# Sliding-window attention and a gated MLP on one core: one explicit order of steps for every engine, and weights loaded by casting DMA

## The chip, the cores and the metric

The kernel runs on one core of one Trainium2 chip. The metric is the device time of one execution in microseconds. Each version was run several times beside the kernel before on the same chip, and only runs in the fast state are compared. A ratio is the mean time of one kernel's fast runs over that of the other's of the same rounds, so it is not quite the ratio of the medians that are quoted, and its 95% interval stands behind it in brackets. The kernel before had medians of 200.6 to 201.8 us in the different calls. So versions are compared by ratio, or by starts and spans within the traces.

Engines are named as in the profile: PE (TensorE matmul), PEld (its weight loads), DVE (VectorE), ACT (ScalarE), POOL (GpSimd), SP (SyncE, which here only issues DMAs).

## The reference, cut to what matters

```python
# q, k, v: (4, 8, 768, 64) float32; n_sink = 4, window = 128
rel  = pos[:, None] - pos[None, :]
keep = (pos[None, :] < n_sink) | ((rel >= 0) & (rel < window))
a    = softmax(where(keep, q @ k.T / 8, -1e9)) ;  x = a @ v        # x: (4, 768, 512)
h    = gelu_tanh(x @ w_in)                                         # w_in: (512, 1024)
u, v = h[..., :512], h[..., 512:]
v_n  = (v - mean(v)) / sqrt(var(v) + 1e-6) * g_ln
v_s  = w_sg @ v_n + b_sg                                           # over the 768 positions
out  = x + (u * v_s) @ w_out                                       # w_out: (512, 512)
```

There are four batches. Each has four pairs of heads, so there are 16 times three inputs of 384 KB each (18.9 MB in all). The weights w_in, w_sg and w_out are 2, 2.25 and 1 MB as float32. The outputs are 6.3 MB.

## The kernel before

For each batch b there is an attention part, pair by pair: cast q, k and v to bf16, transpose on PE (`trp`), scores (`sc`), exponentials on ACT, masks on DVE or POOL, products with v (`av`). Then comes a feed-forward part: `hv` (called MV), `hu` (MU), layer norm of v into `z`, the spatial product `vs` (SP), a gate, and the output `ops`. The spatial product and the output of batch b are mixed with the attention of batch b+1.

```python
def T(b, p):                                   # one pair's inputs: cast, transpose, copy
    for name, src in (("q", q32), ("k", k32)):
        ...
        if name == "k" and b >= 2: nc.scalar.copy(cv, sv)
        else:                      pcast(cv, sv)                 # POOL
        ps = ps_mm.tile([128, NT, 128], BF16, name="trp", tag="mm")
        for t in range(NT): nc.tensor.transpose(ps[:, t, :], ..., iden)
        ...
    pcast(v_sb[b % 2][...], v32...)
...
def load_w_sg(ti):                             # 6 of these; w_in and w_out alike, cast on POOL
    t = wst.tile([128, S], F32, name="wst")    # a pool of 4 buffers
    nc.sync.dma_start(out=t, in_=moe_w_sg[128 * ti:128 * (ti + 1), :])
    r = zpool.tile([128, S], BF16, name="wsg_row")
    nc.vector.tensor_copy(r, t)                # the cast, on DVE
    ...                                        # six transposes on PE, one copy on DVE
...
for b in range(B):
    if b == 0:
        load(1, 0)
        for ti in range(NT): load_w_sg(ti)
        load_vectors(); load(1, 1)
        for c in range(KU): load_w_out(c)
        load(1, 2); load(1, 3)
    for jj in range(NG): MV(b, jj)
    for d in range(KU):
        MU(b, d)
        if b == 0: T(1, d)                     # batch 1's inputs, among batch 0's hu
    if nxt: VS(b + 1)                          # the v_sink product of the next batch, POOL
    su = s_units(b)                            # SP and OUT of batch b
    SK(b + 1, list(range(HP)))                 # sink scores: want all four pairs of b+1
    ...                                        # attention of b+1, with su spread among it
```

The attention of batch 0 is in a fixed order; after it a scheduler orders each engine's instructions.

The softmax here doesn't subtract the row's maximum and nothing guards it: scores larger than these inputs give would overflow.

## Time and profile before

The median was 200.39 us (200.15 to 202.23, three runs). The profiled execution took 202.63 us and spans 200.9 us from its first to its last instruction. To see where it goes, I cut the span at two events per batch, read from the timeline of PE: the first `hv` matmul and the first `vs` matmul.

| stretch | before, us | PE busy in it, us |
|---|---|---|
| start to first hv of batch 0 | 31.2 | 16.6 |
| hv 0 to vs 0 | 33.9 | 23.6 |
| vs 0 to hv 1 | 27.3 | 25.9 |
| hv 1 to vs 1 | 13.0 | 12.0 |
| vs 1 to hv 2 | 29.1 | 26.6 |
| hv 2 to vs 2 | 11.9 | 11.8 |
| vs 2 to hv 3 | 24.1 | 22.8 |
| hv 3 to vs 3 | 10.6 | 10.6 |
| vs 3 to end | 19.9 | 13.8 |

The first two rows stand out: 65 us in which PE is busy for 40. The page of the kernel before shows the same in its 40 slices of 5 us. Each digit is tenths of the slice; PEclk is the granted TensorE clock, DMA the busy share of the DMA engines:

```profile
PE   0458756899067999979988989999999997997992
PEclk9999999999955799999999999999999999999999
DMA  5999993799999502998993002121000122100034
GB/s 171 293 294 329 396 299 136 181 303 319 310 287 299 166 3 64 269 269 254 286 287 64 0 24 84 54 108 52 0 0 5 52 108 100 56 3 2 20 138 157
```

Slice 11 (50 to 55 us) has PE at 0, and then PEclk reads 5, 5, 7. (PEclk also shows 9 where the trace has no clock event yet: the first one is at 16.9 us, and before it six transposes take 0.82 us, as at half clock.) DMA runs at about 300 GB/s up to 65 us, with one dip at 30 to 40 us. The timeline of PE of the kernel before around that hole follows (start, length, line, what, and in brackets the idle time before it and its releaser):

```profile
47.03 2.76 PE L306 MATMUL hu<-xT,w_in_sb 128*128 128x384 bf16 x16
50.69 0.38 PE L213 MATMUL sc<-qT,kT 64*128 64x256 bf16 x3 [0.57 <-ACT uT L148]
55.65 0.82 PE L179 MATMUL trp<-iden,qb 128*128 128x128 bf16 x6 [4.58 <-POOL qb L164]
63.18 0.82 PE L179 MATMUL trp<-iden,kb 128*128 128x128 bf16 x6 [1.09 <-POOL kb L164]
65.07 0.85 PE L319 MATMUL vs<-wsgT,z 128*128 128x384 bf16 x2
```

PE ends batch 0's `hu` before 50 us and waits 4.58 us for an input of batch 1. When it starts again, six transposes take 0.82 us, against 0.50 us when it is warm.

Why the loads are late is seen in the timeline of SP's queue in the kernel before (the length is the time the queue is held by these issues):

```profile
18.30 0.42 SPq L76 DMA_DIRECT2D v_568<-in_v_dram  x1
19.30 16.62 SPq L352 DMA_DIRECT2D wst<-in_moe_w_sg_dram  x6
36.99 0.43 SPq L72 DMA_DIRECT2D q_644<-in_q_dram  x1
39.12 6.30 SPq L364 DMA_DIRECT2D wst<-in_moe_w_out_dram  x4
45.52 0.38 SPq L72 DMA_DIRECT2D q_662<-in_q_dram  x1
```

Six loads of w_sg hold the queue for 16.6 us. The first issue alone takes 7.1 us; 7.4 us pass before the fifth and sixth, which wait for one of four buffers (the queue's own waits there are 3.8 us behind DVE, which makes the casts, and 2.7 us behind the loads before). The inputs of batch 1's second pair stand behind them, and those of the third pair also behind the four loads of w_out.

### The profile page before, as it was taken

What the parts mean: (1) busy time and instruction counts of PE and PEld (TensorE: products, weight loads), DVE (VectorE), ACT (ScalarE), POOL (GpSimd) and SP (SyncE); (2) the same over time, 40 slices, a digit from 0 to 9 for tenths busy, and PEclk for the clock granted to TensorE, in tenths of its full rate; (3) what the DMA queues carried; (4) which work ended last, traced back from release to release, by engine and by line L of the source; (5) the groups of instructions that cost most, each with busy time, mean ns of one, the idle gap of its engine ahead of it and who ended that gap; (6) DMA issues with size and microseconds to landing.
All of it is one profiled execution on the core that took longest, in us unless ns stands there. A gap on an engine that the chain in (4) does not pass through costs nothing.

```text
span 200.9 us, 3839 instructions
## 1 busy us (share of the span) xinstructions
PE 163.7 (81%) x1460; PEld 92.3 (46%) x1460; DVE 140.5 (70%) x269; ACT 112.3 (56%) x131; POOL 110.4 (55%) x173
## 2 busy tenths in 40 slices
PE   0458756899067999979988989999999997997992
PEld 0227533565033566555444446564545655463440
DVE  4148898994855379784756998875759987475653
ACT  2256874557555265758569865646687653761000
POOL 3896597016966689772245995600349651033650
PEclk9999999999955799999999999999999999999999
DMA  5999993799999502998993002121000122100034
GB/s 171 293 294 329 396 299 136 181 303 319 310 287 299 166 3 64 269 269 254 286 287 64 0 24 84 54 108 52 0 0 5 52 108 100 56 3 2 20 138 157
DMA packets 39843, 31.35 MB, mean 156 GB/s; under 512 B 26640, under 2 KB 34832, under 8 KB 39824
## 3 DMA queue, kind: packets, MB, share of 16 engines
q1 hardware_dynamic: 39408, 30.68, 52.5%
q10 hardware_dynamic: 416, 0.43, 0.7%
q8 instruction: 11, 0.18, 0.4%
q14 instruction: 8, 0.07, 0.1%
HBM read 24.81 MB, written 6.29 MB: 155 GB/s over the span
## 4 chain that ended last, share of the span: by engine, by line
PE 31%; DVE 23%; POOL 17%; DMA 11%; issue 8%; ACT 5%; SPq 1%; POOLq 1%; DVEq 0%; ACTq 0%
PE vs L319 10%; DVE pt L221 6%; PE ops L332 6%; DVE z L296 6%; DMA k_646<-in_k_dram 4%; POOL rs L294 4%; PE hv L279 4%; DMA v_1703<-in_v_dram 3%; DVE gtmp L323 3%; PE sc L213 3%; POOL gatedT L326 2%; DMA q_98<-in_q_dram 2%; DVE x_sb L260 2%; POOL kb L164 2%; PE xps L268 2%
## 5 line engine op out<-in xcount | busy, mean ns | idle before, releaser
L326 POOL TENSOR_TENSOR gatedT<-gtmp,uT 128x384 bf16<-128x384 bf16 x32 | 31.4, 984 | 18.1 <-DVE gtmp L323 17.7
L319 PE MATMUL vs<-wsgT,z 128*128 128x384 bf16 x192 | 38.8, 336 | 2.4 <-DVE z L296 1.9
L148 ACT ACTIVATE pt<-sc 128x1024 bf16<-128x1024 f32 (+1 forms) x36 | 32.9, 957 | 6.5 <-PE sc L213 3.6
L323 DVE SCALAR_TENSOR_TENSOR gtmp<-vs,g_sb,b_bc 128x384 bf16<-128x384 f32 x32 | 19.6, 614 | 12.9 <-PE vs L319 12.3
L332 PE MATMUL ops<-w_out_sb,gatedT 128*128 128x512 bf16 x96 | 25.2, 380 | 2.6 <-POOL gatedT L326 2.6
L185 ACT COPY kT<-trp 128x768 bf16<-128x768 bf16 x16 | 12.9, 805 | 23.3 <-PE trp L179 23.3
L319 PEld LDWEIGHTS <-z 128*128 128x128 bf16 x192 | 17.7, 100 | 17.6 <-issue 4.8
L279 PE MATMUL hv<-w_in_sb,xT 128*128 128x512 bf16 x96 | 23.5, 379 | 1.2 <-ACT xT L269 0.9
L213 PE MATMUL sc<-qT,kT 64*128 64x256 bf16 x192 | 19.1, 282 | 4.7 <-ACT pt L148 1.6
L306 PE MATMUL hu<-xT,w_in_sb 128*128 128x384 bf16 x128 | 21.9, 326 | 0.9 <-ACT vt L148 0.9
L290 DVE BATCH_NORM_STATS2 st<-vt 128x6 f32<-128x512 f32 x24 | 15.8, 675 | 9.7 <-ACT vt L148 9.2
L296 DVE TENSOR_SCALAR z<-vt,mv,rs 128x512 bf16<-128x512 f32 x24 | 14.4, 642 | 10.7 <-POOL rs L294 10.6
L221 DVE TENSOR_TENSOR pt<-pt,mask_122 128x1024 bf16<-128x1024 bf16 (+1 forms) x20 | 17.7, 891 | 5.3 <-ACT pt L145 3.9
L269 ACT COPY xT<-xps 128x768 bf16<-128x768 bf16 x16 | 12.9, 804 | 13.8 <-PE xps L268 13.7
L335 DVE TENSOR_TENSOR ot<-ops,x_sb 128x512 f32<-128x512 f32 x24 | 16.3, 687 | 5.1 <-PE ops L332 4.8
L221 DVE TENSOR_TENSOR pt<-pt,mask_127 128x1024 bf16<-128x1024 bf16 x16 | 14.9, 934 | 6.5 <-ACT pt L148 3.4
L292 POOL TENSOR_SCALAR rs<-mv 128x2 f32<-128x2 f32 x12 | 2.3, 193 | 31.1 <-DVE mv L291 30.9
L179 PE MATMUL trp<-iden,qb 128*128 128x128 bf16 x96 | 9.3, 242 | 11.3 <-POOL qb L164 11.2
L260 DVE TENSOR_TENSOR x_sb<-av,rcp 128x384 bf16<-128x384 f32 x32 | 17.6, 556 | 0.9
L183 DVE COPY qT<-trp 128x768 bf16<-128x768 bf16 x16 | 15.1, 944 | 4.3 <-PE trp L179 4.2
L244 PEld LDWEIGHTS <-pt 128*128 128x128 bf16 x192 | 15.2, 100 | 5.4 <-DVE pt L221 3.5
L306 PEld LDWEIGHTS <-w_in_sb 128*128 128x128 bf16 x128 | 12.4, 98 | 9.6 <-issue 1.2
(126 smaller groups left out, 297.8 us busy)
## 6 DMA issues: line engine op xcount, KB each, us to landing
out_dram<-ot SPq DMA_DIRECT2D x24, 256.0 KB, 2.1
wst<-in_moe_w_sg_dram SPq DMA_DIRECT2D x6, 384.0 KB, 5.4
wt<-in_moe_w_in_dram SPq DMA_DIRECT2D x4, 512.0 KB, 7.7
wst<-in_moe_w_out_dram SPq DMA_DIRECT2D x4, 256.0 KB, 4.7
k_100<-in_k_dram ACTq DMA_DIRECT2D x1, 384.0 KB, 4.9
q_98<-in_q_dram SPq DMA_DIRECT2D x1, 384.0 KB, 4.5
v_102<-in_v_dram SPq DMA_DIRECT2D x1, 384.0 KB, 6.3
q_104<-in_q_dram SPq DMA_DIRECT2D x1, 384.0 KB, 6.8
```

What stands on the lines that cost most here:

```text
L148: r = nc.scalar.activation(func=func, **kw)
L213: nc.tensor.matmul(sc[:, hl, 256 * jl:256 * jl + n], kT[b, p][rows, 128 * j:128 * (j + 1)], qT[b, p][rows, 128 * j:128 * j + n], start=Tru ...
L221: nc.vector.tensor_mul(pt[:, :, 0:w], pt[:, :, 0:w], m.unsqueeze(1).to_broadcast([128, 2, w]))
L260: nc.vector.tensor_mul(x_sb[b][:, 3 * half:3 * half + 3, 128 * p:128 * (p + 1)].rearrange("p t (h d) -> p t h d", h=2), av[:, :, :, 0:Dh], ...
L279: nc.tensor.matmul(hp[:, jl, :], xT[b][:, c, 128 * j:128 * (j + 1)], w_in_sb[:, c, d_half:2 * d_half], start=(c == 0), stop=(c == KD - 1))
L296: nc.vector.tensor_scalar(out=z[b][:, 2 * jj + jl, :], in0=vt[:, jl, :], scalar1=mv[:, jl, 0:1], scalar2=rs[:, jl:jl + 1], op0=ALU.subtrac ...
L306: nc.tensor.matmul(hp[:, hf, 0:NH], w_in_sb[:, c, 128 * dc:128 * (dc + 1)], xT[b][:, c, NH * hf:NH * (hf + 1)], start=(c == 0), stop=(c == ...
L319: nc.tensor.matmul(ps[:, 0:NH], z[b][:, si, 128 * dc:128 * (dc + 1)], wsgT[:, si, NH * hf:NH * (hf + 1)], start=(si == 0), stop=(si == NT ...
L323: nc.vector.scalar_tensor_tensor(out=tmp, in0=ps[:, 0:NH], scalar=g_sb[:, dc:dc + 1], in1=b_bc[:, NH * hf:NH * (hf + 1)], op0=ALU.mult, op ...
L326: nc.gpsimd.tensor_mul(gatedT[b, hf][:, dc, :], tmp, uT[b][:, dc, NH * hf:NH * (hf + 1)])
L332: nc.tensor.matmul(ps, gatedT[b, hf][:, dc, 128 * tl:128 * (tl + 1)], w_out_sb[:, dc, :], start=(dc == 0), stop=(dc == KU - 1))
L335: nc.vector.tensor_add(ot, ps, x_sb[b][:, t, :])
```

## The change

The intent: the scheduler is turned off; one list of 713 short words gives each engine's order for the whole program (a word's letter picks the engine, where there is a choice). The weights come by three DMAs issued from POOL that cast float32 to bf16 on the way, so the staging buffers and the casts on engines go. The loads of batch 1 are held until the cast of q of batch 0's last pair, "weights go first". And 32 identity matmuls (WARM) run on PE while it awaits the first q. The list also changes things: three outputs (O, OA, ST 3 to 5) of each of batches 0 to 2 move behind the next batch's first hv; all four `v_sink` products (VS) go to the start.

```diff
+ORDER = """
+Lq00 Lk00 CONST Lv00 Lvs WARM VS0:d VS1:p VS2:p Cq00:p Lq01 Ck00:p Tq00 Lk01 Eq00:a VS3:p Tk00 Ek00:a Lv01 Cv00:p
+...
+Lk03 X011 Ek02:d Cv02:p Lv03 N001 X012 QK020 Iwin KS02:d XT00 X020 M011:d SK02 QK021 Cq03:p M012:d EX00:a AV010
+QK022 M020:d AV011 Ck03:p XS02 Tq03 N010 X021 Tk03 Eq03:d Cv03:p Ek03:a N011 Lq10 Iwsg X022 QK030 KS03:d XT01 M021:d
+...
+M032:d AV030 Lk10 Eq10:d AV031 Lv10 N030 WT0 N031 WT1 WT2 EW0:d XT03 Ck10:p Lq11 EW1:d WT3 EX03:a EW2:d WT4 Lk11
+MV00 EW3:d EW4:d Cv10:p Lv11 MV01 Iwo GV00 Cq11:p WT5 Ck11:p Tk10 EW5:d Tq11 GV01 MV02 BS00 Lq12 Cv11:p Ek10:a Lk12
+...
+KS21:p Cq23:p Ck23:a MV11 GV10 Cq30:p Lk31 Cv30:p O03 Lq32 O04 GV11 BS10 Cv31:p Lk32 MV12 Lv32 BS11 PW10 MU10 GV12
+...
+"""
+    ctx.enter_context(tc.manual_schedule())
...
+    def Iwsg(e):
+        nc.gpsimd.dma_start(out=wsg_rows, in_=moe_w_sg.rearrange("(c p) f -> p c f", p=128))   # f32 -> bf16
...
+    def behind_weights(d, b, p):
+        if (b, p) == (1, 0):
+            tc.add_manual_dep(d.ins, last["Cq", 0, HP - 1].name, ..., reason="weights go first")
...
+    def WARM(e):
+        for _ in range(32):
+            nc.tensor.matmul(ps[:, 0:128], iden, iden, start=True, stop=True)
...
-    def load_w_sg(ti): ...          # staging, cast on DVE
-    def load_w_in(c): ...           # staging, cast on POOL
-    def load_w_out(c): ...
...
+    for word in ORDER.split():
+        what, _, e = word.partition(":")
+        name = what.rstrip("0123456789")
+        steps[name](e, *(int(c) for c in what[len(name):]))
```

In a word, digits are batch, pair, and block. L loads, C casts, T transposes, E copies to SBUF, X exponentials, M masks, EX copies x transposed, WT and EW are the transposes of w_sg and their copies, I are the casting loads, and the other names are as above.

## The prediction

> **What bounds the kernel now.** Reading the span (200.9 us) by the starts of the five stretches, from the timeline (first matmul into hv per batch): 37.3, 92.6, 134.5, 170.4, end 200.9. So the head takes 37 us, then batches cost 55, 42 and 36 us, and the tail 30. The work is the same each time, so the first two periods carry about 19 and 6 us that the third does not.
> Why: the queue of loads (SP) is shared by inputs and weights, and loads stand behind weight buffers: in the windows DMA moves only 145 GB/s at 30-35 us against about 300 around it. In the wait list POOL's qb waits once for 10.7 us behind PE, and PE's transposes wait 11.2 us for qb. PE is busy 0.49 of 5 us at 50-55 us. The granted clock then reads 0.50 at 55-65 and 0.69 at 65-70. Batch 1's transposes come only at 55.7-63.2 us. In the second period POOL and ACT wait for v_1583, v_1703 and k_1701.
> In the third period, PE is busy 23.8 of 25 us (145-170): close to PE-bound.
>
> **What the change does.**
> - Removes: six wsg casts on DVE (3.8 us), four w_in and four w_out casts on POOL (7.9 us). Six of 16 kT/qT copies net leave DVE (16 to 10, 0.94 us each, 5.7 us); ACT gains six copies but sheds three kb casts; POOL sheds four small ks_sink products, gains three kb casts.
> - Adds: three casting loads issued by POOL, 32 identity matmuls at the start.
> - Moves: everything. Loads of batch 1 go after the weights, but no load waits for a weight staging buffer; half of each batch's output matmuls and adds move into the next feed-forward stage, where DVE has room.
>
> **Costing by stage.**
> - Head: 37.3 to about 37. DVE work there falls by about 4 us, but POOL now makes two v_sink tiles (1.06 us each) before the first qb; their vs_all lands at about 7.2 us against q at 5.3, so the start slips by up to 4 us. The spatial weight transposes stand before the first hv on PE and wait for the casting load (estimate 34-36 us: 11 MB at 300 GB/s). No gain.
> - First period: 55 to about 38.5. Inputs through batch 1 are about 15 MB, at 300 GB/s in by 51-53 us instead of 60; the 5 us hole and the half-clock stretch (11.6 us of PE busy at 55-70, so about 5 us) go.
> - Second: 42 to 37.5, less load waiting, outputs deferred.
> - Third: 36 to 34.5. Tail: 30 to 30.
>
> Sum 177.5 us; predicted 178 us, range 171 to 188. Chances: faster 0.94, same 0.04, slower 0.02.
>
> **Warm-up matmuls.** The Trainium skill, "TensorE: Matmul & The Clock Gate" (HAM clock gate), says that the array runs at half rate until about 3.4 us of activity, and again after an idle window. The trace agrees: six transposes take 0.82 us at 6-15 us, 0.50 from 19 us, 0.82 again at 55.7 after the idle 5 us. I give the warm-up under 1 us: PE is idle again before the first qb, and loads bound the head.
>
> **What would show it.** Right: first hv matmuls near 37, 75, 113, 148 us; no clock dip near 50-70; DMA at about 300 GB/s without the hole to 52 us; DVE busy about 10 us lower.
> **What would make it wrong.** Casting loads slower than 300 GB/s, or sharing the DMA engines unfairly (the Trainium skill, "DMA: Bandwidth & Descriptors", arbitration: round robin by packet; no run yet shows it), so that batch 1's inputs or wsg come late and PE, in fixed order, stands before the weight transposes and cools; a fixed order that blocks an engine behind a late item; descriptor writing on POOL costing microseconds.

## More of the kernel before

(In batch 0 of the kernel before, six of the 24 `hv` matmuls come early, from 31.18 us; the other 18 run from 37.32 us on.)

The clock events of the trace put the half clock at 54.5 to 68.1 us. The first `vs` comes only at 65.07; the sink scores, which want all four pairs of batch 1, stand before it.

The q of the third pair (q_662) landed at 50.96 us, just as PE ran out of work, and was cast only from 54.59 us. POOL's timeline of the kernel before shows what stood in front of that cast:

```profile
50.59 1.37 POOL L164 TENSOR_SCALAR w_out_sb<-wst 128x512 bf16<-128x512 f32 x2
52.75 0.62 POOL L164 TENSOR_SCALAR w_out_sb<-wst 128x512 bf16<-128x512 f32 x1
54.01 0.62 POOL L164 TENSOR_SCALAR w_out_sb<-wst 128x512 bf16<-128x512 f32 x1
54.59 1.00 POOL L164 TENSOR_SCALAR qb<-q_662 128x768 bf16<-128x768 f32 x1
```

Between these lines POOL does small steps of the layer norm and of the sink scores. The fourth pair is alike: its k (k_670) landed at 56.5 us and was cast at 62.3. So in the hole it is the order of work on POOL that comes last.

## The result, and the profile after

The changed kernel took 185.81 us in the median (185.32 to 186.25, four runs), against 200.64 us of before in the same rounds: ratio 0.9248 [0.9188, 0.9308]. The profiled run spans 184.3 us. It lies in the predicted range, 7.8 us above the predicted 178. The profiled run of the kernel before was 2.0 us above its median and that of the changed kernel 0.4 us, so the spans differ by 16.6 us, the medians by 14.8; about 1.8 us of the table below are the choice of runs.

| stretch | before | after | difference |
|---|---|---|---|
| start to hv 0 | 31.2 | 40.6 | +9.4 |
| hv 0 to vs 0 | 33.9 | 14.0 | -19.9 |
| vs 0 to hv 1 | 27.3 | 23.6 | -3.7 |
| hv 1 to vs 1 | 13.0 | 15.0 | +2.0 |
| vs 1 to hv 2 | 29.1 | 22.9 | -6.2 |
| hv 2 to vs 2 | 11.9 | 14.6 | +2.7 |
| vs 2 to hv 3 | 24.1 | 21.6 | -2.5 |
| hv 3 to vs 3 | 10.6 | 13.4 | +2.8 |
| vs 3 to end | 19.9 | 18.7 | -1.2 |
| sum | 200.9 | 184.3 | -16.6 |

Up to the first spatial product 10.5 us were gained (65.1 to 54.6), and 6.1 us after it. Put another way: PE is idle for 37.2 us before and 24.9 us after (span less busy time), and its busy time fell from 163.7 to 159.4 us; 12.3 and 4.3 make the 16.6. The busy time fell although WARM adds 3.6 us. PE was busy for 9.8 us at half clock between 54.5 and 68.1 us before and for 5.8 us in the dip of the kernel after, which makes some 2 us of it (an estimate, half of the difference); the rest is not explained by these views.

The page of the kernel after, the same rows as before:

```profile
PE   6047578869989999999999998999989899999971
PEclk9999957999999999999999999999999999999999
DMA  5999699999999968899850022000400120013044
GB/s 159 305 292 275 82 231 199 272 258 279 280 279 307 294 187 223 250 272 316 206 194 0 4 82 91 3 0 0 174 0 0 71 104 4 0 57 114 2 171 171
```

The hole at 50 to 55 us and the half clock behind it are gone. There is a new dip of the clock in slices 6 and 7 (the clock events say half from 23.5 to 30.3 us), a dip of DMA to 82 GB/s in the fifth slice (18.4 to 23.0 us), and a 0 in the second slice of PE.

Three things in the head are new. First, what follows are the waits of the kernel after within its first 12 us (engine, line, releaser: total us, times, longest):

```profile
PE trp L243 <- POOL qb L115: 5.7, 1, 5.7
POOL v_sink_114 L261 <- DMA vs_all<-in_v_dram: 4.4, 1, 4.4
```

POOL must do two v_sink products before the first cast, and they wait for `vs_all`. The first cast starts at 9.9 us, against 5.33 us in the kernel before. The timeline of PE of the kernel after shows what became of the warm-up:

```profile
1.42 3.59 PE L223 MATMUL warm<-iden 128*128 128x128 bf16 x32 [1.42 <-POOL iden masks.py:199]
10.75 0.82 PE L243 MATMUL trp<-iden,qb 128*128 128x128 bf16 x6 [5.73 <-POOL qb L115]
```

PE is idle 5.73 us after it, and the first transposes take 0.82 us, as cold as in the kernel before. In this trace the clock events show no full clock before 16.6 us, so WARM did not even lift it here.

Second, POOL's timeline of the kernel after, and third, DVE's in the same stretch:

```profile
18.46 0.97 POOL L158 DMA_DIRECT2D w_in_sb<-in_moe_w_in_dram  x1
19.46 0.84 POOL L115 TENSOR_SCALAR qb<-q_318 128x768 bf16<-128x768 f32 x1
20.26 0.83 POOL L115 TENSOR_SCALAR kb<-k_351 128x768 bf16<-128x768 f32 x1
21.06 0.83 POOL L115 TENSOR_SCALAR v_sb_117<-v_358 128x768 bf16<-128x768 f32 x1
21.83 0.88 POOL L161 DMA_DIRECT2D wsg_rows<-in_moe_w_sg_dram  x1
```

```profile
18.45 3.85 DVE L308 TENSOR_TENSOR pt<-pt,mask_104 128x1024 bf16<-128x1024 bf16 x2
22.22 0.18 DVE L358 RECIPROCAL rcp<-av 128x6 f32<-128x6 f32 x1
```

The second of the two masks took 3.25 us (from 19.05) where the other 35 of this trace take 0.55 to 1.36: it began under the DMA issue and ended, at 22.30, only when the three casts in a row were over. PE has only 1.87 us of work in 20 to 25 us and cools. The load of w_sg is issued at 21.83 us, and PE meets the wait for it (1.6 us, `PE wps L423 <- DMA wsg_rows`), which ends at about 38.5 us, 16.7 us after the issue. Only then come the transposes of w_sg, and behind them the first hv, at 40.57.

The queues of the page, kernel before and then after (queue, kind: packets, MB, share of the 16 engines' time):

```profile
q1 hardware_dynamic: 39408, 30.68, 52.5%
```

```profile
q1 hardware_dynamic: 37392, 25.17, 48.9%
q0 software_dynamic: 1840, 2.75, 9.0%
```

The casting loads are counted by the bf16 bytes that they write; the page's bytes read from HBM are the same (24.81 MB). In engine time, 52.5% of 200.9 us is 105.5 us, and 48.9% plus 9.0% of 184.3 is 106.7 us: casting in the DMA saves no DMA time.

### The profile page after: what moved, and what is told of

The parts are those of the page before. It is cut to its first block, busy times and chain, and to the rows that moved or that the text cites. A ratio compares the mean times of both kernels' runs of the same rounds, so it can differ in the third digit from the quotient of the medians.

```text
span 184.3 us, 3837 instructions
## 1 busy us (share of the span) xinstructions
PE 159.4 (87%) x1492; PEld 96.0 (52%) x1492; DVE 132.9 (72%) x262; ACT 113.3 (61%) x134; POOL 108.6 (59%) x166
## 3 DMA queue, kind: packets, MB, share of 16 engines
q1 hardware_dynamic: 37392, 25.17, 48.9%
q0 software_dynamic: 1840, 2.75, 9.0%
HBM read 24.81 MB, written 6.29 MB: 169 GB/s over the span
## 4 chain that ended last, share of the span: by engine, by line
PE 35%; DMA 18%; POOL 18%; DVE 10%; ACT 10%; issue 5%; POOLq 1%; SPq 0%; ACTq 0%
DMA wsg_rows<-in_moe_w_sg_dram 9%; PE vs L432 7%; POOL gatedT L445 7%; PE hu L411 6%; PE hv L378 5%; PE ops L452 5%; DMA v_1413<-in_v_dram 4%; PE sc L289 4%; DMA vs_all<-in_v_dram 3%; ACT pt L300 3%; DVE z L403 2%; ACT qT L117 2%; POOL qb L115 2%; POOL pt L313 2%; DVE ot L457 2%
## 5 line engine op out<-in xcount | busy, mean ns | idle before, releaser
L300 ACT ACTIVATE pt<-sc 128x1024 bf16<-128x1024 f32 (+1 forms) x48 | 44.3, 960 | 9.0 <-PE sc L289 6.9
L445 POOL TENSOR_TENSOR gatedT<-gtmp,uT 128x384 bf16<-128x384 bf16 x32 | 29.4, 923 | 15.0 <-DVE gtmp L438 14.2
L432 PE MATMUL vs<-wsgT,z 128*128 128x384 bf16 x192 | 35.4, 326 | 0.3 <-DVE ot L457 0.3
L289 PE MATMUL sc<-qT,kT 64*128 64x256 bf16 x192 | 17.5, 279 | 5.3 <-DVE kT L117 2.1
L411 PE MATMUL hu<-xT,w_in_sb 128*128 128x384 bf16 x128 | 21.6, 326 | 0.0
L313 POOL TENSOR_SCALAR_AFFINE_SELECT pt<-pt 128x256 bf16<-128x256 bf16 x24 | 15.4, 662 | 5.8 <-ACT pt L300 5.8
L457 DVE TENSOR_TENSOR ot<-ops,x 128x512 f32<-128x512 f32 x24 | 16.1, 683 | 3.6 <-PE ops L452 3.5
L359 DVE TENSOR_TENSOR x<-av,rcp 128x384 bf16<-128x384 f32 x32 | 17.8, 557 | 1.1
L117 ACT COPY qT<-trp 128x768 bf16<-128x768 bf16 x13 | 10.3, 807 | 12.5 <-PE trp L243 12.5
L417 ACT ACTIVATE uT<-hu 128x768 bf16<-128x768 f32 x16 | 13.0, 810 | 6.6 <-PE hu L411 6.5
L384 ACT ACTIVATE vt<-hv 128x1024 f32<-128x1024 f32 x12 | 12.1, 1023 | 7.9 <-PE hv L378 7.8
L403 DVE TENSOR_SCALAR z<-vt,mv,rs 128x512 bf16<-128x512 f32 x24 | 13.6, 610 | 2.4 <-POOL rs L397 2.3
## 6 DMA issues: line engine op xcount, KB each, us to landing
wsg_rows<-in_moe_w_sg_dram POOLq DMA_DIRECT2D x1, 1152.0 KB, 16.7
```

Source lines behind the costliest of these rows:

```text
L117: return nc.scalar.copy(out_, in_) if e == "a" else nc.vector.tensor_copy(out_, in_)
L289: nc.tensor.matmul(sc[:, hl, 256 * jl:256 * jl + n], T["Ek", b, p][rows, 128 * j:128 * (j + 1)], T["Eq", b, p][rows, 128 * j:128 * j + n], ...
L300: nc.scalar.activation(out=pt[:, :, 0:w], in_=T.pop(("QK", b, p, g))[:, :, 0:w], func=AF.Exp, scale=scale)
L313: nc.gpsimd.affine_select(out=d0, in_=d0, compare_op=ALU.is_ge, fill=0.0, base=0, pattern=[[0, 2], [1, 128]], channel_multiplier=-1)
L411: nc.tensor.matmul(hp[:, hf, 0:NH], w_in_sb[:, c, 128 * dc:128 * (dc + 1)], T["xT", b][:, c, NH * hf:NH * (hf + 1)], start=(c == 0), stop= ...
L432: nc.tensor.matmul(ps[:, 0:NH], T["z", b][:, si, 128 * dc:128 * (dc + 1)], wsgT[:, si, NH * hf:NH * (hf + 1)], start=(si == 0), stop=(si = ...
```

## The experiments

All the variants gave correct results. They are given by stretch starts: the first hv (MV) of batches 0 and 1 and the first vs (SP) of batch 0, in us from the span's start.

| version | median | ratio to before | MV 0 | SP 0 | MV 1 | span |
|---|---|---|---|---|---|---|
| before | 200.6 | 1 | 31.2 | 65.1 | 92.4 | 200.9 |
| after | 185.8 | 0.9248 | 40.6 | 54.6 | 78.2 | 184.3 |
| b_sw: before, casting loads only | 199.9 | 0.9919 | 30.9 | 62.8 | 92.2 | 198.0 |
| a_hw: after, without casting loads | 190.2 | 0.9435 | 42.1 | 56.7 | 82.2 | 187.8 |
| a_vs: VS1 to 3 after the w_sg issue | 182.6 | 0.9056 | 37.1 | 51.1 | 74.9 | 180.8 |
| a_nowarm: no WARM | 185.5 | 0.9216 | 39.4 | 53.4 | 77.2 | 183.1 |
| a_vs2: VS1 to 3 still later | 183.9 | 0.9132 | 37.6 | 51.6 | 75.4 | 181.6 |
| a_vs2_fill: a_vs2 and filler on PE | 186.4 | 0.9253 | 40.3 | 54.5 | 78.3 | 184.1 |
| a_nodefer: outputs not deferred | 190.0 | 0.9427 | 40.6 | 54.6 | 80.8 | 188.9 |
| a_sk: sink scores of batch 1 early again | 187.2 | 0.9286 | 40.5 | 57.2 | 80.0 | 185.9 |
| a_vs2_wt: a_vs2, w_sg transposes behind hv | 183.1 | 0.9077 | 32.8 | 51.5 | 75.3 | 181.1 |
| b_late: before, batch 1's last pairs later | 201.4 | 0.998 | 31.0 | 49.4 | 88.1 (one matmul; most from 91.7) | 199.6 |
| b_fill: before, filler in PE's hole | 198.3 | 0.9828 | 31.3 | 59.9 | 82.1 (one matmul; the others from 87.9) | 195.1 |
| a_best: a_vs2_wt spread out, w_out later | 183.2 | 0.9108 | 32.2 | 51.0 | 74.5 | 181.2 |

### Which part of the change: order or loads

b_sw puts only the casting loads into the kernel before; a_hw takes only them out of the changed one.

```diff
 b_sw (kernel before)
-    load_w_in / load_w_sg / load_w_out with staging tiles and casts on DVE and POOL
+    Iwin() behind the transposes of the third pair, Iwsg() behind those of the fourth, Iwo() behind batch 0's attention
 a_hw (changed kernel)
-    Iwin, Iwsg, Iwo
+    SP loads of w_in, w_sg, w_out into float32 tiles; casts Cwi:p, Cws:d, Cwo:p before their first use
```

> The kernel before, with one part of the change alone: w_in, w_sg and w_out come by three casting loads issued by POOL, with no staging tiles and no casts; the order stays the scheduler's. Theory 'loads' (most of the 14.8 us comes from batch 1's inputs no longer standing behind weight buffers): 186 to 192 us, batch 1's last input cast before 58 us, no half clock around 60 us. Rival 'order' (the fixed order of steps is what gains): 197 to 201 us.

> The changed kernel with the opposite undo: the fixed order stays, but the weights come as fp32 by SP into staging tiles as before (four 3 KB buffers per partition for w_sg and w_out) and are cast by POOL (w_in, w_out) and DVE (w_sg). Theory 'loads': 192 to 199 us, most of the gain lost. Rival 'order': 185 to 189 us.

Measured: loads alone 0.9919 [0.9887, 0.9952], order alone 0.9435 [0.9395, 0.9475], both 0.9248. So the casting loads give some 1.6 us on the old order and some 3.7 us on the new one; the order gives 11 us without them and 13.5 with them. At the first hv of batch 1 it is clearer still: against the kernel before it comes 0.3 us earlier with the loads alone, 10.2 us with the order alone and 14.2 us with both. In b_sw the hole stays: PE is busy 1.39 of 5 us at 55 to 60 us, and the clock reads 0.50 at 60 to 65. Two lines of PE's timeline in b_sw:

```profile
38.60 1.03 PE L357 MATMUL wps<-iden,wsg_rows 128*128 128x128 bf16 x8 [5.44 <-DMA wsg_rows<-in_moe_w_sg_dram]
58.25 0.80 PE L177 MATMUL trp<-iden,kb 128*128 128x128 bf16 x6 [3.40 <-DVE qT L181]
```

PE's longest wait at the old place (3.4 us, ending at 58.25) is now behind a DVE copy of a transposed pair, so removing the jam of the load queue, and with it the casts of w_out on POOL, did not remove the hole. And the casting load of w_sg opens a new hole of 5.4 us in the head, so the 1.6 us are a balance of the two, not the worth of the jam alone. In a_hw, in turn, two loads of w_sg still hold back batch 1's inputs until 38.9 us on the same queue, and no hole of 2 us or more stands behind it (the clock is halved once, from 38.3 to 41.7 us). The idea that the late loads explain the first period by themselves fell.

### What the hole in the kernel before was worth

Two edits to the kernel before go at the hole by itself. b_late moves batch 1's last two pairs and its sink scores behind the first scores; b_fill keeps PE awake in the hole with 22 useless products.

```diff
 b_late
-            if b == 0: T(1, d)
+            if b == 0 and d < 2: T(1, d)
 ...
+            if b == 0 and p == 0:      # behind the first score blocks of batch 1
+                au += [T(1, 2), T(1, 3), SK(1, all pairs)]
 b_fill
-            if b == 0: T(1, d)
+            if b == 0 and d < 2: T(1, d)
+            if b == 0 and d == 3:      # behind batch 0's last hu
+                fl = ps_mm.tile([128, 512], F32, name="fill", tag="mm")
+                for _ in range(22): nc.tensor.matmul(fl, iden, mask1, start=True, stop=True)
+                # then T(1, 2), T(1, 3), issued after the last of these
```

> The kernel before with one thing of the new order in batch 1: the transposes of its last two pairs and its sink scores are asked for after the first score blocks, beside the spatial products, so that the scheduler no longer puts them ahead of the first spatial product. Theory 'it is the place of waiting work on PE that made the hole at 50-65 us': first spatial product near 54 to 57 us in place of 65, no half clock or a shorter one, 192 to 197 us. Rival 'the hole is lateness of the loads': 199 to 202 us.

> The kernel before with 22 identity products of 512 columns (4.7 us of PE) put into the hole that begins at 50 us, ahead of the transposes of batch 1's last two pairs, to keep the clock up. It takes no wait away. Theory 'a good part of the loss at 55-68 us is the half clock that the hole brings': clock 1.00 there, 195 to 198 us. Rival 'the waits themselves are the loss': 199.5 to 202 us.

b_late: 0.998 [0.9924, 1.0036], no gain. The first spatial product starts 15.6 us earlier (49.4), but then it waits for z on DVE (up to 2.3 us), PE waits 3.2 us for the cast of a late pair at 64 us, and the clock is halved twice, at 53.6 to 60.4 and 63.8 to 67.2 us. One matmul of batch 1's hv comes 4.3 us earlier, but most of them, from 91.70, only 0.7 us; at MV 2 the lead is 1.4. My theory that the early demand for batch 1's inputs costs the time on its own fell: the work merely waits elsewhere.

b_fill: 0.9828 [0.9751, 0.9906], about 3.5 us (runs from 196.8 to 199.6, between the ranges of the theory and of its rival; by the 2% rule the verdict is unclear, though the interval lies below 1). The profiled run was the fastest of the four. The clock row of the page of b_fill has no dip:

```profile
PEclk9999999999999999999999999999999999999999
```

The first hv of batch 1 comes 10.3 us earlier than in the kernel before, but that is a single matmul which the scheduler put in front, as PE's timeline of b_fill shows:

```profile
82.07 0.38 PE L279 MATMUL hv<-w_in_sb,xT 128*128 128x512 bf16 x1
87.87 3.39 PE L279 MATMUL hv<-w_in_sb,xT 128*128 128x512 bf16 x14
```

The others start 4.5 us earlier (87.87 against 92.41). The first vs of batch 0 is 5.2 us earlier, that of batch 1 6.1 us, MV 2 5.7 us and the end 5.8 us, so in this run the lead of the filled hole is kept to the end. (The scheduler also moved other work of batch 1 in b_fill, on POOL and in SP's queue, so that the filling was not quite changed by itself.)

So the order is worth more than the filling of the hole. Against b_fill's trace, the changed kernel is 5.3 us earlier at the first vs of batch 0, and it gains 0.8 us more up to the first vs of batch 1, 3.7 us from there to that of batch 2, loses 0.3 up to that of batch 3 and gains 1.4 behind it. SP's queue holds batch 2's last loads behind an output store in the kernel before (66.4 to 78.4 us) and in b_fill (63.6 to 72.0 us); in the changed kernel 11 of the 12 loads leave before the first store, against 9. Whether that gains time is not shown: no run changed it by itself.

### The late start of POOL and the stuck mask

a_vs moves VS1 to VS3 from the start to just after the issue of w_sg; a_vs2 moves them behind the cast of batch 1's first q; a_vs2_fill adds ten identity matmuls before each pair's first scores to a_vs2.

```diff
-... WARM VS0:d VS1:p VS2:p Cq00:p ... VS3:p ... Iwsg X022 ... Cq10:p ... Ck10:p
+... WARM VS0:d Cq00:p ... Iwsg VS1:p VS2:p VS3:p X022 ... Cq10:p ... Ck10:p        # a_vs
+... WARM VS0:d Cq00:p ... Iwsg X022 ... Cq10:p VS1:p VS2:p VS3:p ... Ck10:p        # a_vs2
```

> The changed kernel with POOL's three v_sink products for batches 1 to 3 moved from the start to just after the w_sg load is issued. Theory 'late start' (POOL waits for vs_all until 7.2 us and casts the first q only at 9.9 us, which delays the whole head and the two casting loads): 181.5 to 183.5 us, first hv matmul near 37 us, w_in issued near 14.5 us instead of 18.5, no DMA gap at 18-20 us. Rival 'head is bound by the bytes of w_sg or by the cold clock': 185 to 186.5 us although the first q is cast near 5.4 us.

> As a_vs, but the three v_sink products stand later, between the casts of batch 1's first q and k, so that POOL falls idle right after it issues the w_sg load. In a_vs one 128x768 mask product on DVE took 3.84 us from 20.43 us, under the w_sg issue and the three products that ran back to back behind it. Theory 'a gapless run on POOL holds DVE's two-input product': that mask falls to 0.6 to 1.4 us and the kernel to 179.5 to 181.5 us. Rival 'the writing of the casting load's descriptors holds it': the mask stays at 3 to 4 us, 182 to 183 us.

> a_vs2 plus ten identity matmuls ahead of the first score block of each pair of batch 0, where PE waits for kT, so that the clock stays up. Theory 'the cold clock costs the head': clock 1.00 at 8-18 us and 25-30 us, and 0.5 to 1.5 us less than a_vs2. Rival 'the head is held by DVE and by loads': same as a_vs2 within 0.4 us, or more by the fillers' own time.

a_vs: 0.9056 [0.9028, 0.9084], 182.56 us, the shortest time of all. MV 0 comes 3.5 us earlier and the span is 3.5 us shorter, so what the start gains here is kept to the end. In a_vs there is again one stuck mask: 3.84 us from 20.43, begun under the w_sg issue (19.83, 0.88 us), while three v_sink products ran from 20.74 to 23.84. Hence a_vs2, where nothing follows the issue on POOL. Its DVE timeline:

```profile
19.73 1.75 DVE L308 TENSOR_TENSOR pt<-pt,mask 128x1024 bf16<-128x1024 bf16 x3
```

Three masks in 1.75 us, so the stuck mask is gone. Yet a_vs2 is not faster than a_vs (0.9132 [0.9072, 0.9192], MV 0 at 37.6). The attention is done earlier, and PE stands longer before w_sg. The waits from 24 to 42 us of a_vs2, then of a_vs2_fill:

```profile
PE wps L423 <- DMA wsg_rows<-in_moe_w_sg_dram: 3.3, 1, 3.3
```

```profile
PE wps L426 <- DMA wsg_rows<-in_moe_w_sg_dram: 4.8, 1, 4.8
```

In a_vs2 the clock is halved behind that wait, at 33.9 to 37.3 us. a_vs2_fill holds the clock full from 9.8 to 26.9 us, and makes it worse: 0.9253. Its w_sg issue slips from 19.74 to 21.33 us with POOL's casts, w_sg lands at 36.5, PE waits 4.8 us for it and is cold from 26.9 to 40.5. So in these two the landing of w_sg decides, which follows its place in POOL's order. That is not so in every variant: in a_vs w_sg lands at 34.1 and PE does not wait for it, and in a_nodefer and a_sk below, which keep the changed kernel's head, it lands at 36.6 and 36.4, PE waits for no load there, and MV 0 still comes at 40.6 and 40.5; in those two traces the clock is full only from 30.9 and 30.8 us. The attention on PE and the landing of w_sg end close together in this head.

a_nowarm drops WARM from the changed kernel:

```diff
-... Lvs WARM VS0:d ...
+... Lvs VS0:d ...
```

> The changed kernel without the 32 identity matmuls at the start. Theory 'they are wasted' (PE idles 5.7 us between the last of them and the first transpose, and the first transposes take 0.82 us as in the kernel before): 185.3 to 186.3 us, no change. Rival 'they keep the clock from falling': 187 us or more.

Measured 0.9216 [0.9174, 0.9257]: no loss. The warm-up has no value here, since 5.7 idle us follow it. Whether the 32 products lift the clock at all differs from trace to trace: a_hw, a_vs, a_vs2_wt and a_best show full clock from 4.2 to 4.8 us, and where POOL starts early (the last three) the first transposes then take 0.51 us; the changed kernel, a_vs2, a_vs2_fill, a_nodefer and a_sk, with the same 32 products, show it from 9.8 us at the earliest.

### The deferred outputs and the sink scores

a_nodefer puts the last three outputs of batches 0 to 2 back before the next batch's first hv; a_sk puts batch 1's last transposes and sink scores back before batch 0's first spatial product.

```diff
 a_nodefer, for b = 0, 1, 2
-... MV(b+1)0 ... MV(b+1)1 ... Ob3 ... Ob4 ... Ob5 OAb3 ... STb5
+... Ob3 Ob4 OAb3 STb3 Ob5 OAb4 STb4 OAb5 STb5 MV(b+1)0 ...
 a_sk
-... Tq13 SP000 X100 Lk20 Eq13:d KS12:p Tk13 Cv13:p ... Ek13:d ... KS13:p ... SK10 ... XS10
+... Tq13 Eq13:d Tk13 KS12:p Ek13:d KS13:p SK10 SP000 X100 XS10 Lk20 Cv13:p ...
```

> The changed kernel with the last three output rows of batches 0 to 2 done before the next feed-forward stage, not inside it. Theory 'PE-bound, so deferral only moves work between stages': 185 to 187.5 us, feed-forward stages about 2.5 us shorter and the mixed stages about as much longer. Rival 'deferral fills idle PE time', as the prediction had it: 189 us or more.

> The changed kernel with one thing of the old order in batch 1: the transposes of the last pair and the sink scores of all four pairs stand on PE before the first spatial product, not after it. Theory 'the old order made PE wait for batch 1's last load before it began the spatial products, and cooled it': PE idles 2 to 5 us near 53 us, 188 to 191 us. Rival 'the place of the sink scores doesn't matter': 185 to 186.5 us.

a_nodefer: 0.9427 [0.9358, 0.9495], 4 us slower. MV 1 is 2.6 us later, and MV 2 and MV 3 by 5.3 and 6.4 us; the tail gives 1.8 us back. The stage table says where. What follows are the windows from vs 1 to hv 2, of the kernel after and then of a_nodefer (window, its length, busy us and instructions of PE, PEld, DVE, ACT, POOL, clock, DMA share, GB/s):

```profile
93.20:116.08 22.88, 22.10 (x263) 14.12 (x263) 19.31 (x37) 18.01 (x23) 16.68 (x27) 1.00 0.19 65
```

```profile
92.80:121.33 28.53, 24.88 (x272) 15.11 (x275) 21.94 (x41) 21.51 (x27) 20.92 (x33) 1.00 0.14 46
```

The 12 output matmuls are 2.6 us of PE (12 starts, 0.216 us apart), and this stage is longer by that; but PE is also idle for 3.65 us in it, against 0.78. The feed-forward stage gives back only the 2.6 us (12.0 against 14.6 us, PE without a gap in both). So the deferral takes away no work of PE: it takes away its idle time. Where that lies is shown by PE's timeline of a_nodefer at the front of that stage:

```profile
94.61 1.77 PE L432 MATMUL vs<-wsgT,z 128*128 128x384 bf16 x8 [0.98 <-DVE z L403]
98.48 0.39 PE L273 MATMUL scs<-qT,ks_sink 128*128 128x512 bf16 x1 [1.00 <-POOL ks_sink L255]
```

With the wait of 0.50 us before another sink score and one of 0.12 us for z, these are 2.6 of the 3.65 us; the last outputs themselves run without a gap (118.7 to 121.3 us). In the changed kernel the same matmuls start without waiting for z or ks_sink, which fits that the deferred outputs keep PE busy in the feed-forward stage while DVE and POOL finish those. The rival, that PE is busy on either side and the move is neutral, fell.

a_sk: 0.9286 [0.9222, 0.935], 1.4 us slower by the medians, and the intervals overlap. SP 0 is 2.6 us later but MV 1 only 1.8, so the sink scores' place matters little.

### Clearing the head

a_vs2_wt takes the transposes of w_sg out from before the first hv; a_best spreads the v_sink products to their own batches and issues w_out later as well (at 51.5 us, in a_vs2_wt at 37.7).

```diff
 a_vs2_wt, on a_vs2
-... WT0 ... WT1 WT2 EW0:d ... WT4 ... MV00 EW3:d EW4:d ... WT5 ... EW5:d
+... MV00 ... MV01 ... MV02 WT0 WT1 BS00 EW0:d EW1:d ... MU00 WT2 WT3 ... MU01 WT4 WT5 ...
 a_best, on a_vs2_wt
-... Cq10:p VS1:p VS2:p VS3:p ...  MV01 Iwo ...  Ck13:p Tq13
+... Cq10:p VS1:p ...  MV01 ...  Ck13:p Iwo Tq13 ...  PW12 VS2:p ...  PW22 VS3:p
```

> a_vs2 with the transposes of w_sg (and their copies) moved from ahead of the first hv matmuls to behind them, between the hv and hu groups. In a_vs2 PE idles 3.3 us for w_sg until 33.96 us and comes out of it at half clock. Theory 'the landing of w_sg is what holds the head once the v_sink products are out of the way': first hv near 32 to 34 us, 178 to 181.5 us. Rival 'batch 1's inputs, which land near 52 us whatever the order, hold the next stage': the first hv comes earlier but the first spatial product not, 182.5 to 184 us.

> The changed kernel with three moves together: the v_sink products of batches 1 to 3 out of the start (batch 1's after batch 1's first cast, the others with their own batch's casts), the w_sg transposes behind the first hv product, and the casting load of w_out one step later, so that its 1 MB does not stand in front of batch 1's last inputs. Last run with the first two: first hv at 32.75, first spatial product at 51.54, 183.1 us. Theory 'bytes in front of batch 1's last inputs hold the first spatial product once the head is freed': first hv near 32 us, first spatial product near 48 to 50 us, 178 to 181.5 us. Rival 'the last vectors' work on VectorE and GpSimd holds it, whatever the loads do': first spatial product at 51 us or later, 182 to 183.5 us.

a_vs2_wt: MV 0 comes at 32.75 us, 4.8 us earlier than in a_vs2, but SP 0 at 51.54, the same. 0.9077 [0.9025, 0.9129]. a_best: MV 0 at 32.19, SP 0 at 50.95, 183.17 us, 0.9108 [0.9071, 0.9144]. Eight microseconds of lead on the changed kernel at MV 0 become 3.6 at SP 0 and about 2.6 at the end. The loads do not hold SP 0, as the first theory of a_best had it; that one fell. In a_best PE waits only once from 44 us to the first vs, 0.7 us for POOL's qb, whose q had landed at 45.6. What fills the stretch from MV 0 to SP 0 is work of PE. What follows are the windows of that stretch, of a_best and then of the kernel after (as above: window, length, busy us of PE, PEld, DVE, ACT, POOL, clock, DMA share, GB/s):

```profile
32.19:50.95 18.76, 16.82 (x138) 10.15 (x137) 10.98 (x24) 12.13 (x15) 11.65 (x18) 0.92 1.17 300
40.57:54.59 14.02, 13.52 (x109) 8.14 (x107) 10.05 (x22) 11.30 (x14) 11.27 (x18) 1.00 1.16 279
```

It is 4.7 us longer: 1.8 us are transposes of w_sg that used to stand before MV 0 (36 in the stretch, before 6), some 1.5 us are the half clock from 32.2 to 35.1 us (an estimate, half of the 2.9 busy us in it), and 1.4 us are more idle time (1.9 against 0.5 us, in a_best 1.3 and 0.7 us for POOL's qb). So part of the lead at MV 0 was only work that moved across the mark. DVE and POOL of a_best, their timelines:

```profile
47.45 0.99 DVE L117 COPY wsgT<-wps 128x768 bf16<-128x768 bf16 x2
48.36 3.43 DVE L403 TENSOR_SCALAR z<-vt,mv,rs 128x512 bf16<-128x512 f32 x4
51.71 0.94 DVE L117 COPY qT<-trp 128x768 bf16<-128x768 bf16 x1
```

```profile
47.62 0.19 POOL L395 TENSOR_SCALAR rs<-mv 128x2 f32<-128x2 f32 x1 [1.01 <-DVE mv L391]
49.55 1.00 POOL L115 TENSOR_SCALAR qb<-q 128x768 bf16<-128x768 f32 x1
```

DVE has no gap from 42.4 us on, and its last z ends at 51.79, after the first `vs` has begun; POOL waits in its fixed order for a statistic of DVE and only then casts the last pair, whose transposes stand before `vs` on PE. So the last vectors' work is not what PE waited for, beyond that 0.7 us, but it would hold a first vs that came much earlier: PE, DVE and POOL end close together. The versions a_vs, a_vs2_wt and a_best all beat the changed kernel by 1.4 to 1.9% of the time before, and their intervals overlap or touch. a_vs is the best of them: four runs at 182.49 to 182.61 us, with three words of the list moved.

## Why the prediction was right, and where its sizes were off

The call (faster by over 2%, 171 to 188 us) held. The point was 7.8 us low in the median. Against the span of the trace, 184.3, the sum 177.5 misses 6.85 us. It goes like this, with the terms as the prediction put them:

| term | predicted | measured | off by |
|---|---|---|---|
| head, to the first hv | 37 | 40.6 | +3.6 |
| first period | 38.5 | 37.6 | -0.9 |
| second | 37.5 | 37.9 | +0.4 |
| third | 34.5 | 36.2 | +1.7 |
| tail | 30 | 32.05 | +2.05 |

- **What bounds the kernel before: right in the place, with one misreading.** The hole, the jam of the load queue and the half clock are where it said. But one start was misread: the first hv of batch 0 is at 31.18 us, not at 37.3. Six matmuls come early, and the other 18 from 37.3 on. Between first matmuls the head grew by 9.4 us and the first period shrank from 61.2 to 37.6; counted from 37.3 the head grew by 3.3. The sum of the two is not touched by that. And the hole was put down to late loads, while the q that PE waited for had landed 3.6 us before POOL cast it.
- **First period, "55 to about 38.5": right in size.** The hole and the half clock went, as said. The cause was put too much on the loads, so that the size is in part luck: the four kernels with and without each part give the casting loads 1.6 to 3.7 us and the order 11 to 13.5, and at MV 1 the loads alone 0.3 us. The prediction had batch 1's inputs in by 51 to 53 us instead of 60; the last of them landed at 54.7 instead of 58.2, just as the first vs had begun (54.6), which in the new order no longer stands behind the sink scores of all four pairs.
- **Head, "No gain": mis-sized by 3.6 us.** The step that failed is setting the later start ("the start slips by up to 4 us") off against 4 us less DVE work, and the estimate that w_sg lands at 34 to 36 us. It landed at about 38.5. a_vs undoes the late start alone, and MV 0 goes to 37.10, the predicted 37. The first cast slipped by 4.5 us, and the slip counted nearly in full: in a_vs w_sg is issued 2.0 us and w_in 2.5 us earlier, and MV 0 comes 3.5 us earlier.
- **Third period and tail: mis-sized by 3.75 us together.** The deferred outputs hand 2.6 us of PE from each batch to the next. Only the first period is relieved of them without getting any; the second and third give and take; the tail takes. I had counted relief in the third and left the tail at 30. In a_nodefer the stretch from MV 3 to the end is 30.3 us, in the changed kernel 32.05.
- **"DVE busy about 10 us lower": 7.6** (140.5 to 132.9). The stuck mask alone puts 2.6 us back (3.25 less about 0.65, an estimate).
- **"No clock dip near 50-70": right,** but a new one came at 23.5 to 30.3 us, which I had named only as a risk.
- **"DMA at about 300 GB/s without the hole to 52 us": partly wrong.** It is 82 GB/s, with the engines busy for 0.63 of the time, in 18.4 to 23.0 us, where batch 1's first load waits for a cast on POOL and the w_sg issue stands behind three casts.
- **Warm-up, "under 1 us": right;** a_nowarm shows none.
- **"Sharing the DMA engines unfairly": it happened, in a small way.** From the issue of w_sg to its landing (21.83 to 38.5 us) the DMA view of the kernel after counts 2.10 MB written by the casting queue, which is about 4.2 MB of float32 read (an estimate, twice the bf16 bytes), and 1.81 MB on the plain queue; inputs of 384 KB that mostly land in about 6 us otherwise took 16.6 to 17.2 us. The Trainium skill, "DMA: Bandwidth & Descriptors" (arbitration), says that a DMA engine takes the queues in turn, a packet at a time; the view counts 1249 packets of the casting queue and 2839 of the plain one, so, if these are the packets that the page means, one for one is not what it shows.

The Trainium skill, "TensorE: Matmul & The Clock Gate" (HAM clock gate), gives two states, half and full, with a window of about 3.4 us. The traces agree: each hole of over 4 us has the half clock behind it, six transposes at 0.82 instead of 0.50 us, and the stretches of half clock last 3.4 us or a multiple of it: 3.4 in a_vs2 (33.9 to 37.3), 6.8 in the kernel after (23.5 to 30.3), 13.6 in the kernel before (54.5 to 68.1). Shorter holes had it too: 3.3 us in a_vs2, 2.6 in a_vs, and 2.1 in the kernel after, amid little work.

What stays open: why a mask that begins under a DMA issue of POOL loses every turn to the POOL instructions behind it, while other masks take turns with POOL; and how much of the 11 us of the order belongs to which of its many moves. The two that were undone alone (the deferral, 4 us; the sink scores, about 1 us) leave about half unassigned, and the parts need not add.

## What to carry to other kernels

A hole in the matmul engine need not be due to the load that its wait leads back to: here the load had landed 3.6 us before another engine, busy with other work, took it up. Compare landing and use before changing the loads. Filling the hole brought 1.7%, the whole order 7.5%. In a fixed order, every early item on an engine is paid by all that stand behind it: three unneeded products at POOL's start cost 3.5 us at the end, and a load's issue is such an item too. A stage's first instruction is a poor mark where a scheduler or an edit can move single pieces: when a stage's start comes earlier and its end does not, count the work that moved across the mark (here 1.8 us of transposes) and the clock, before looking for an engine that holds it.

## What the Trainium skill lacked or had wrong

- "SBUF — State Buffer" (SBUF: two separate sides) says that the port pair shared by DVE and GpSimd is an exclusive lock and the loser blocks for the other's whole instruction, and (Who interferes with whom) that a DVE instruction with two SBUF inputs, as the mask is, contends with a GpSimd instruction that reads SBUF. The runs show a longer block: a DVE mask, 0.55 to 1.36 us elsewhere in the changed kernel, begun under a DMA issue of POOL, lasted over three POOL instructions in a row (3.25 us in the changed kernel, 3.26 us in a_nowarm, a_nodefer and a_sk, which keep that order, 3.84 us in a_vs). Where no such run of POOL work followed an issue (a_vs2), or where POOL issued no load (a_hw), no mask took over 1.51 us. The page does not say that the block can pass on from instruction to instruction.
- "DMA: Bandwidth & Descriptors" (SWDGE vs HWDGE vs iDMA) says that a cast during DMA is for SWDGE alone, and agrees with the change; it lacks what it costs: the profile counts such loads by the bytes written (2.75 MB here), and the total DMA engine time was not lower than with float32 staging (106.7 against 105.5 us).
- The same page (queues, rings and completion order: arbitration) lacks how a casting load and plain loads share the engines: here 2.10 MB written, about 4.2 MB read (an estimate), to 1.81 MB in 16.7 us, and 16.6 to 17.2 us for a 384 KB input.
- "TensorE: Matmul & The Clock Gate" has nothing on the worth of filler products inside a kernel: 32 at the start gave nothing (0.9216 without them, 0.9248 with), 22 in the hole of the kernel before gave 1.7%, and ten before each pair of a_vs2 cost 1.2% of the time before (0.9132 to 0.9253).
